# Offsets for the gate and rounding points of prepared weights, units 12 to 108

## The chip, the cores and the metric

The kernel runs on one core of one Trainium2 chip. The metric is device time in microseconds (us) for one execution. The engines that matter here are TensorE (PE, with its weight load PEld), VectorE (DVE), ScalarE (ACT), GpSimd (POOL) and SyncE (SP), which issues most of the transfers.

## The reference, cut to what matters

```python
mod = (_silu(c) @ w_mod).reshape(c.shape[0], 6, 1, -1)
sa, ca, ga, sb, cb, gb = (mod[:, i] for i in range(6))
h = _layernorm(x) * (1 + ca) + sa
q = (h @ wq).reshape(1, 2048, 32, 128)          # 32 heads, D = 576
k, v = last 512 rows of the caches, 16 heads, each used by two query heads
o = softmax(q k^T / sqrt(128)) v
x = x + ga * (o @ wo)
h = _layernorm(x) * (1 + cb) + sb
x = x + gb * (((h @ W_gate) masked where > 0) * (h @ W_up)) @ W_down      # F = 4608
```

Everything is float32 in and out.

## The kernel before

**Precision.** A float32 operand of a matmul is split into a rounded part "hi" (type fp32r) and the remainder "lo", also fp32r, and a product is three matmuls: hi·hi, lo·hi, hi·lo. So every operand costs a rounding (ACT: `scalar.copy`) and a subtraction (POOL: `tensor_sub`). The function `split` (lines 181 to 183) does this for weights; the code calls it the *cut* of a weight.

**Units.** The attention stage is a list of 128 *units*, one for each head and block of 512 queries. Eight units in a row belong to one key/value head (four blocks, two query heads); the last five key/value heads are visited twice with two blocks each, so four units in a row. TensorE works through unit u in a fixed order: the scores s of u (12 matmuls of 512 columns, L496 to L498, in the order hi·hi, lo·hi, hi·lo), the q projection of unit u+1 (14 matmuls of 512, L424), a *piece* of the output projection wo (12 matmuls of 288 columns, L660), probabilities times v for the first half of u-1 (6 of 512, L633 to L635), for the second half (6), and another wo piece (12). The other engines serve this:

- DVE: maxima of s (tile t, L501), the subtraction of the maximum (p, L591), the remainder of the next q (qlo, L480), half of the softmax sum (ks, L606), the scaling of the attention output (`o_mul`, L641, tile rb).
- ACT: the next q's rounded part (qhi, L476), the exponential (L593), the rounded p (hi, L577), the rounded output (ohi, L645).
- POOL: the rest of the softmax sum (ks, L609, two instructions), the remainder of p in two halves (lo, L600, named lo<unit>_0 and lo<unit>_1 where both halves are meant apart), the remainder of the output (olo, L649).

Each engine runs its own instructions in program order, so where a piece of side work is written decides what it stands ahead of. Within a unit POOL's fixed order is: ks of u (two instructions), lo of u (two), olo of an earlier unit (one), then ks of u+1. PE needs lo of u in the next unit's two pv halves, and olo of an odd unit, with the odd head's wo weights, in the wo piece at the end of a unit.

**Side work.** The weights of coming units are prepared meanwhile: q weights (tile wA), keys and values (kv), wo weights (raw tile roga, cut tile woga). Each has a load on SP's queue into a ring of two raw buffers, then, for wo alone, a *gate* (DVE multiplies by the row mrow, L223), then the cut (ACT copy, POOL subtraction L183). Because the raw ring has two buffers, a load is let go only when the cut two loads before it has read its buffer. Weights of the key/value heads 12 to 15 are prepared early too and parked in DRAM (`park...`), from where they are reloaded on a visit (`againq`, `againk`, `againo` in the trace). The modulation vectors are also summed beside the units, one part at a time (`m3.0` to `m5.4`, DVE, tile macc, L128 and L130).

**Their order.** Side work is not written into the unit's code. Each piece is a *step*: a name, a time and a function. Unit u is the time span 10u to 10u+9, and the unit's code calls `run(u, k)` at eleven fixed points, which executes every step whose time has come:

```python
def step(name, t, fn, *args):
    sched.append((t + PLAN.get(name, 0), len(sched), fn, args))
...
    step(name + ".l", hook(q - gap), pr[0])
    if len(pr) > 2:
        step(name + ".g", hook(q - 1), pr[1])
    step(name + ".c", t, pr[-1])
...
def run(u, k):
    t = 10 * u + k
    while sched and sched[-1][0] <= t:
        fn, args = sched.pop()[2:]
        fn(*args)
```

The suffix says which part it is: `.l` load, `.g` gate, `.c` cut (for the m steps, the summing). A name such as `q9.c` is the cut of the q weights of head 9, `k` and `v` count key/value heads, `o` the wo weights of a head. Before the change all these weights use the points 0, 4, 6 and 9 of a unit only. On POOL three gaps follow from the points: k = 6, 7, 8 falls between ks and lo of the unit (called A below), k = 9 and the next unit's 0 to 3 between lo and olo (B), and later points after olo and ahead of the next ks (C).

Of the kernel before, what the change touches and what calls it, by code (L numbers as in the profile page):

```python
# [23 lines left out]
EPS = 1e-5  # L24
SCALE = float(P) ** -0.5
H2 = D // 2
PLAN = {'a1.st0': -14, 'a1.nm0': -15, 'a1.st1': -14, 'a1.nm1': -15, 'a1.st2': -14, 'a1.nm2': -15, 'a1.st3': -14, 'a1.nm3': -15, 'a1.rs': -15, 'a1.tr0': -15, 'a1.af0': -11, 'a1.tr1': -15, 'a1.af1': -15, 'a1.tr2': -15, 'a1.af2': -15, 'mods': -3}
CFG = {'a0': (('s', 'vvp', 'vvv'), ('m', 'aap', 'avp'), ('w', 'aav')), 'a1': (('w', 'aap', 'vap'), ('m', 'vvp', 'vvv'), ('s', 'avp'))}
PE0, PE1, MLP0 = 4, 1, 8
# [5 lines left out]
def kernel(  # L35
# [106 lines left out]
    def mod_row(j, r, plus):  # L142
# [7 lines left out]
        for h in range(2):  # L150
            nc.tensor.matmul(ps[h][:, :H2], ones, m[:, h * H2:(h + 1) * H2], start=True, stop=True)
        for h in range(2):
            nc.scalar.activation(r[:, h * H2:(h + 1) * H2], ps[h][:, :H2], AF.Copy, bias=plus,
                                 scale=1.0)
# [117 lines left out]
    class LayerNorm:  # L272
# [4 lines left out]
        def stats(self, i):  # L277
# [6 lines left out]
            for h in range(2):  # L284
                nc.vector.bn_stats(bn[:, h, :], a[:, h * H2:(h + 1) * H2])
            nc.vector.bn_aggr(self.xn[-1][:, i, :], bn)
# [143 lines left out]
    def keep(key, t):  # L430
        akeep[key] = k = dr.tile(list(t.shape), F32R, name="ak%s%d" % key)
        nc.scalar.dma_start(k.bitcast(F32), t.bitcast(F32))
# [50 lines left out]
    st_, t5, pt, hi_, lo_, bc, rb, ks_, pvps, done, o, bps = ({} for _ in range(12))  # L483
# [167 lines left out]
    def down_piece(his, los, ws, i, qt, nm, pool=None, seed=None):  # L651
# [3 lines left out]
        for half in range(2):  # L655
            cs = slice(half * H2, (half + 1) * H2)
            n = 0
            for hi, lo, w in zip(his, los, ws):
                for a, b in ((hi, 0), (hi, 1), (lo, 0)):
                    nc.tensor.matmul(ps[:, half, :H2], a[:, sl], w[b][:, cs],  # L660
                                     start=(n == 0 and seed is None), stop=(n == 5),
# [4 lines left out]
        def add():  # L666
            adds[i] += 1
            if seed is not None:
                nc.scalar.copy(av, ps[:, :, :H2])
                return  # L670
# [255 lines left out]
    def w_later(s, xx, where):  # L926
        pool, tag, w = where
        st = {}
        eng = nc.gpsimd
        terms = terms_of(s, WTERMS)  # L930

        def get(dst, i, j):
            nc.sync.dma_start(dst, wlay0[i, j, :, xx, :])

        def begin():
            for x in "ab":
                st[x] = pool.tile([P, w], F32, tag=tag, name=f"w{x}_{s}_{xx}")[:, :384]
            for x, term in zip("ab", terms):
                get(st[x], *term[1:])

        def comb(i):
            x, y = st["a"], st["b"]
            eng.tensor_tensor(x, x, y, op=ALU.add if terms[i][0] == "+" else ALU.subtract)
            if i + 1 < len(terms):
                get(st["b"], *terms[i + 1][1:])

        def cut():
            a = st["a"]
            hi = st["b"].bitcast(F32R)
            nc.scalar.copy(hi, a)  # L950
            nc.gpsimd.tensor_sub(hi[0:32, 256:], a[0:32, 256:], hi[0:32, 256:].bitcast(F32))
            lo = a[:, :256].bitcast(F32R)
            nc.gpsimd.tensor_sub(lo, a[:, :256], hi[:, :256].bitcast(F32))
            stores.append((wkeep[0, s][:, xx, 0:3, :].rearrange("p t n -> p (t n)"), hi))
            stores.append((wkeep[0, s][:, xx, 3:5, :].rearrange("p t n -> p (t n)"), lo))

        return [begin] + [lambda i=i: comb(i) for i in range(1, len(terms))] + [cut]
# [326 lines left out]
    sched = []  # L1284

    def step(name, t, fn, *args):
        sched.append((t + PLAN.get(name, 0), len(sched), fn, args))

    HOOK = (0, 4, 6, 9)
    e = 10 * NU  # L1290
# [1 line left out]
    def hook(q):  # L1292
        return 10 * (q // 4) + HOOK[q % 4]

    def prep(name, t, pr, gap=2):
        q = 4 * (t // 10) + HOOK.index(t % 10)
# [4 lines that stand above are left out]
# [93 lines left out]
    step("wo1.g", 23, po[1])  # L1394
    step("wo1.c", 32, po[2])
    def sk(t, key, d, k):
        step("keep", t, lambda: keep(key, d[k][2] if key[0] == "o" else
                                     d[k] if key[0] == "q" else d[k][:, 0:8, :]))

    def weights(g, d):  # L1400

        h = 2 * g
        return [(("q", h), d["q"], prep5(d["q"], h, wq, "wA")), (("k", g), d["k"], prep_kv(d["k"], g, 0)),
                (("q", h + 1), d["q"], prep5(d["q"], h + 1, wq, "wA")),
                (("v", g), d["v"], prep_kv(d["v"], g, 1)), (("o", h), d["o"], prep_out(d["o"], h, wo, "ga")),
                (("o", h + 1), d["o"], prep_out(d["o"], h + 1, wo, "ga"))]

    live = {"q": wqs, "k": ks, "v": vs, "o": wos}
# [4 lines left out]
    for i in range(1, len(VIS)):  # L1413
        g, qbs = VIS[i]
        B = 10 * UNITS.index((g, qbs[0], 2 * g))
        if g in early or g in seen:
            for key, t in zip((("q", 2 * g), ("k", g), ("q", 2 * g + 1), ("v", g), ("o", 2 * g),
                               ("o", 2 * g + 1)), (-30, -20, -14, 0) + ((-4, -4) if i > first + 1 else (6, 34))):
                step("again", B + t, again, key, live[key[0]], key[1],
                     key[0] == "o" and key[1] % 2 and i > first and (i - first) % 2 == 0)  # L1420
        else:
            for (key, d, pr), t in zip(weights(g, live), (-31, -20, -14, 0, 9, 34)):
                prep(key[0] + str(key[1]), B + t, pr, 6 if t == 34 else 4)
                if any(v[0] == g for v in VIS[i + 1:]):
                    sk(B + t + 12, key, d, key[1])
        seen.add(g)
    for i in range(1, first):
        B = 80 * i
        for c, t, gap, a in (("q", 16, 5, 0), ("kv", 24, 5, 1), ("o", 44, 6, 2)):
            if parks[c] and i > a:  # L1430
                key, d, pr = parks[c].pop(0)
                prep("park", B + t, pr, gap)
                sk(B + t + 9, key, d, key[1])
    assert not any(parks.values())
    for i in range(15):
# [150 lines left out]
    def after(t):  # L1586
        return next(x for x in calm if x >= t)

    t = 546
    for s in ("P1", "P2", "P4", "P7", "P5", "P6", "P3"):  # L1590
        for xx in range(2):
            for fn in w_later(s, xx, (xp, "xm", 640)):
                step("w.l", t, fn)
                t = after(t + 8)
            step("w.e", t, flush_stores)
    assert t < 1040, t
# [177 lines left out]
```

## Time and profile before

| What | Value |
|---|---|
| device time, median of 3 | 2859.7 us (2857.88 to 2862.28) |
| the profiled execution: its own time | 2857.6 us |
| its span in the trace | 2855.8 us |
| granted TensorE clock, mean | 0.998 |
| PE busy | 2815.0 us, 99% |
| PEld busy | 2449.5 us, 86% |
| DVE busy | 2246.8 us, 79% |
| POOL busy | 2123.8 us, 74% |
| ACT busy | 1476.7 us, 52% |

The span covers the program's instructions; the execution's own time is 1.8 us longer. Busy shares are means over the whole program, its attention stage (units 0 to 127) and its MLP stage. A share of 99% for PE counts matmuls whose modelled ends overlap, so short waits are better seen from the starts of successive matmuls.

### The profile page before, as it was taken

The page shows a single profiled execution, that of the slowest core. Times are in us where ns is not written, and L with a number is a line of the kernel's source. Part 1 is how long each engine was busy: PE and PEld are TensorE (multiplying, and loading weights), DVE is VectorE, ACT ScalarE, POOL GpSimd, SP SyncE. Part 2 cuts the span into 40 slices and gives each one's busy share as a digit, 9 for nine tenths or more (in the row PEclk, how much of TensorE's full clock was granted, in tenths as well). Part 3 has the DMA queues.
Part 4 walks back from the last instruction along what each step waited for, and adds up shares of the span by engine and source line. Part 5 has one row for each costly group of instructions (what it writes and reads, how often), then busy time and mean ns, then how long its engine had stood idle before and what let it go on. Part 6 is the DMA issues. An engine that isn't in the chain of part 4 may idle for free.

```text
span 2855.8 us, 41174 instructions
## 1 busy us (share of the span) xinstructions
PE 2815.0 (99%) x15006; PEld 2449.5 (86%) x15006; DVE 2246.8 (79%) x3384; ACT 1476.7 (52%) x2105; POOL 2123.8 (74%) x1564
## 2 busy tenths in 40 slices
PE   6999999999999999999999999999999999999999
PEld 5788888888888888888888888888888888888888
DVE  7899999999889998888889756676677466666666
ACT  5766666666766666666656444444444122222221
POOL 5688888888899989877778766788777356656653
PEclk9999999999999999999999999999999999999999
DMA  4012132222232213312243456666667844444442
GB/s 163 24 45 79 65 106 85 83 82 100 95 104 94 92 62 131 105 70 80 68 155 139 150 213 229 231 240 231 234 234 261 338 165 154 155 155 159 159 154 106
DMA packets 164506, 399.57 MB, mean 140 GB/s; under 512 B 15056, under 2 KB 62160, under 8 KB 164304
## 3 DMA queue, kind: packets, MB, share of 16 engines
q1 hardware_dynamic: 132912, 284.69, 29.9%
q10 hardware_dynamic: 31392, 112.26, 10.0%
q8 instruction: 118, 1.93, 0.3%
q14 instruction: 84, 0.69, 0.1%
HBM read 271.16 MB, written 154.57 MB: 149 GB/s over the span
## 4 chain that ended last, share of the span: by engine, by line
PE 83%; DVE 6%; POOL 5%; issue 2%; ACT 2%; DMA 2%; SPq 0%; ACTq 0%; DVEq 0%; POOLq 0%
PE gu L1016 26%; PE wo L660 12%; PE qps L424 11%; PE md L660 8%; PE st_P L1118 6%; PE s L498 3%; PE s L497 3%; PE s L496 3%; PE pv L635 3%; PE pv L634 3%; PE pv L633 3%; POOL lo L600 2%; DVE t L501 1%; DVE p L591 1%; POOL wop L795 1%
## 5 line engine op out<-in xcount | busy, mean ns | idle before, releaser
L600 POOL TENSOR_TENSOR lo<-p,hi 128x1024 fp32r<-128x1024 f32 x256 | 610.6, 2406 | 1.1 <-ACT hi L577 1.1
L609 POOL TENSOR_TENSOR ks<-ks,p 128x512 f32<-128x512 f32 x256 | 351.7, 1374 | 238.7 <-DVE ks L606 135.5
L501 DVE TRANSPOSE_TENSOR_REDUCE t<-s 128x32 f32<-128x1024 f32 x256 | 313.8, 1239 | 85.9 <-PE s L498 76.6
L1016 PE MATMUL gu<-hop_B,wop 128*128 128x512 f32 x1512 | 375.0, 391 | 0.2 <-POOL wop L795 0.2
L1016 PEld LDWEIGHTS gu<-hop_B,wop 128*128 128x128 f32 x1512 | 274.9, 188 | 51.1 <-POOL wop L795 0.9
L1016 PE MATMUL gu<-hop_T,wop 128*128 128x512 f32 x1260 | 316.1, 391 | 0.0
L424 PE MATMUL qps<-hTa,wA 128*128 128x512 f32 x1288 | 312.9, 394 | 3.1 <-DVE hTa L372 1.6
L660 PE MATMUL wo<-woga,ohi 128*128 128x288 f32 x1472 | 298.8, 295 | 2.0 <-POOL woga L183 1.4
L591 DVE TENSOR_TENSOR p<-s,mb 128x1024 f32<-128x1024 f32 x246 | 290.3, 1219 | 4.2
L424 PEld LDWEIGHTS qps<-hTa,wA 128*128 128x128 f32 x1288 | 244.5, 190 | 56.6 <-DVE hTa L372 3.2
L476 ACT ACTIVATE qhi<-qps 128x512 fp32r<-128x512 f32 x128 | 76.4, 597 | 366.9 <-PE qps L424 358.4
L660 PEld LDWEIGHTS wo<-woga,ohi 128*128 128x128 f32 x1472 | 245.9, 188 | 18.8 <-POOL woga L183 3.4
L1016 PEld LDWEIGHTS gu<-hop_T,wop 128*128 128x128 f32 x1260 | 227.8, 188 | 39.0
L577 ACT CAST hi<-p 128x1024 fp32r<-128x1024 f32 x256 | 259.5, 1042 | 1.5
L660 PE MATMUL md<-wogb,hhi 128*128 128x288 f32 x1272 | 256.9, 295 | 0.4 <-DVE acc L671 0.4
L593 ACT ACTIVATE p<-p 128x1024 f32<-128x1024 f32 x246 | 249.5, 1051 | 13.7 <-DVE p L591 13.4
L671 DVE TENSOR_TENSOR acc<-md,acc 128x576 f32<-128x576 f32 x159 | 119.9, 755 | 160.4 <-PE md L660 159.8
L660 PEld LDWEIGHTS md<-wogb,hhi 128*128 128x128 f32 x1272 | 210.9, 188 | 12.6 <-DVE acc L671 1.4
L1127 DVE TENSOR_TENSOR acc<-st_P,acc 128x576 f32<-128x576 f32 x160 | 121.1, 757 | 127.9 <-PE st_P L1118 127.9
L660 PE MATMUL wo<-woga,olo 128*128 128x288 f32 x736 | 217.8, 296 | 1.3 <-POOL olo L649 1.2
L660 PE MATMUL md<-wogb,hlo 128*128 128x288 f32 x636 | 187.5, 295 | 0.0
L649 POOL TENSOR_TENSOR olo<-rb,ohi 128x512 fp32r<-128x512 f32 x128 | 167.4, 1308 | 15.2 <-ACT ohi L645 15.0
(283 smaller groups left out, 7095.3 us busy)
## 6 DMA issues: line engine op xcount, KB each, us to landing
wop<-wk_P SPq DMA_DIRECT2D x133, 640.0 KB
wk_P<-wop ACTq DMA_DIRECT2D x119, 640.0 KB
wr<-wlay SPq DMA_DIRECT2D x68, 384.0 KB
rogb<-wd SPq DMA_DIRECT2D x68, 288.0 KB
againq<-akq SPq DMA_DIRECT2D x18, 640.0 KB
rwA<-wq SPq DMA_DIRECT2D x32, 320.0 KB
wlay<-wg SPq DMA_DIRECT2D x36, 256.0 KB
roga<-wo SPq DMA_DIRECT2D x32, 288.0 KB
```

The costliest lines, as they stand in the source:

```text
L424: return [lambda i=i, a=a, b=b: nc.tensor.matmul(ps, a, b, start=(i == 0), stop=(i == n - 1)) for i, (a, b) in enumerate(ops)]
L501: nc.vector.tensor_reduce(t5[u][:, 2 * h:2 * h + 2, :].rearrange("p k b -> p (k b)"), t.rearrange("p k (b j) -> p (k b) j", j=32), axis=AX ...
L577: nc.scalar.copy(hi_[u, h], pt[u, h])
L591: nc.vector.tensor_tensor(p, t, bc[u][:, None, :].to_broadcast([P, 2, 512]), op=ALU.subtract)
L593: nc.scalar.activation(p, p, AF.Exp, bias=0.0, scale=1.0)
L600: nc.gpsimd.tensor_sub(lo_[u, h], pt[u, h], hi_[u, h].bitcast(F32))
L609: nc.gpsimd.tensor_tensor(ks_[u], ks_[u], p[:, j, :], op=ALU.add)
L649: nc.gpsimd.tensor_sub(olo[u], o.pop(u), ohi[u].bitcast(F32))
L660: nc.tensor.matmul(ps[:, half, :H2], a[:, sl], w[b][:, cs], start=(n == 0 and seed is None), stop=(n == 5), skip_group_check=seed is not None)
L1016: nc.tensor.matmul(ps, a, c, start=s not in heir(m) and i == 0 and s not in seeds_of(m), stop=i == len(ops) - 1, skip_group_check=True)
L1118: nc.tensor.matmul(ps[:, j, :H2], x[:, sl], w[:, y, :], start=n == 0 and not second, stop=n == 2, skip_group_check=True)
L1127: nc.vector.tensor_tensor(t, ps[:, :, :H2], t, op=ALU.add)
```

## The change

One table and one term are added. The table OFF has 103 entries, one for each of the gates and cuts of the weights prepared in units 12 to 108 and of the m3 to m5 sums; each entry moves one step by -3 to +10 tenths of a unit. Other edits of the diff give distinct names to steps (reloads, stores to DRAM, the later combinations of MLP weights) that have no entry in the table, so loads, stores, reloads and copies keep their times. No instruction is added or removed.

```diff
+OFF = {'parkq25.c': -2, 'm4.2.c': 1, 'parkq27.c': -1, 'm4.1.c': 10, 'parkq26.c': 7, 'k3.c': 2, ...
 PLAN = {'a1.st0': -14, ...
...
     def step(name, t, fn, *args):
-        sched.append((t + PLAN.get(name, 0), len(sched), fn, args))
+        sched.append((t + PLAN.get(name, 0) + OFF.get(name, 0), len(sched), fn, args))
...
-        step("keep", t, lambda: keep(key, d[k][2] if key[0] == "o" else
+        step(f"keep{key[0]}{key[1]}_{int(t >= 1000)}", t, lambda: keep(key, d[k][2] if key[0] == "o" else
...
-                step("again", B + t, again, key, live[key[0]], key[1],
+                step(f"again{i}{key[0]}{key[1]}", B + t, again, key, live[key[0]], key[1],
...
-                prep("park", B + t, pr, gap)
+                prep(f"park{key[0]}{key[1]}", B + t, pr, gap)
...
-                step("w.l", t, fn)
+                step(f"w{s}{xx}.{t}", t, fn)
```

What this does to an engine's order is seen from the instructions themselves. On POOL, in units 33 and 34 (the number after ks, lo and olo is the unit; wA_27 are the q weights of head 27, kv13_0 the keys of key/value head 13), before:

```order
L649 TENSOR_TENSOR olo31_4856<-rb31_4755,ohi31_4854 128x512
L609 TENSOR_TENSOR ks33_4881<-ks33_4881,p33_1_4871 128x512 x2
L183 TENSOR_TENSOR wA_27_4885<-rwA_27_4734,wA_27_4885 128x640
L600 TENSOR_TENSOR lo33_0_4915<-p33_0_4868,hi33_0_4874 128x1024
L600 TENSOR_TENSOR lo33_1_4917<-p33_1_4871,hi33_1_4910 128x1024
L649 TENSOR_TENSOR olo32_4923<-rb32_4877,ohi32_4921 128x512
L183 TENSOR_TENSOR kv13_0_4982<-rkv13_0_4796,kv13_0_4982 128x512
L609 TENSOR_TENSOR ks34_5010<-ks34_5010,p34_1_5000 128x512 x2
```

The same engine and place after the change (lines of the changed kernel are one higher):

```order
L650 TENSOR_TENSOR olo31_4856<-rb31_4755,ohi31_4854 128x512
L184 TENSOR_TENSOR wA_27_4871<-rwA_27_4734,wA_27_4871 128x640
L610 TENSOR_TENSOR ks33_4884<-ks33_4884,p33_1_4874 128x512 x2
L601 TENSOR_TENSOR lo33_0_4915<-p33_0_4868,hi33_0_4877 128x1024
L601 TENSOR_TENSOR lo33_1_4917<-p33_1_4874,hi33_1_4910 128x1024
L650 TENSOR_TENSOR olo32_4923<-rb32_4880,ohi32_4921 128x512
L184 TENSOR_TENSOR kv13_0_4967<-rkv13_0_4796,kv13_0_4967 128x512
L610 TENSOR_TENSOR ks34_5010<-ks34_5010,p34_1_5000 128x512 x2
```

The cut wA_27 has moved from gap A (between ks33 and lo33) to gap C (ahead of ks33).

On DVE, in unit 34 (macc4 is a part of the m4 sum, roga_9 the gate of the wo weights of head 9, rb33 the scaling `o_mul` of unit 33), before:

```order
L606 TENSOR_TENSOR ks34_5010<-p34_0_4995 128x512
L641 TENSOR_TENSOR rb33_5006<-pv33_4985,rb33_5006 128x512
L130 SCALAR_TENSOR_TENSOR macc4_3917<-wm4_3_4888,sT_133,macc4_3917 128x576
L223 TENSOR_TENSOR roga_9_4919<-roga_9_4919,mrow2_892 128x576
L501 TENSOR_REDUCE t5_35_5054<-s35_0_5047 128x32
```

And after:

```order
L607 TENSOR_TENSOR ks34_5010<-p34_0_4995 128x512
L131 SCALAR_TENSOR_TENSOR macc4_3884<-wm4_3_4888,sT_133,macc4_3884 128x576
L642 TENSOR_TENSOR rb33_5006<-pv33_4985,rb33_5006 128x512
L224 TENSOR_TENSOR roga_9_4919<-roga_9_4919,mrow2_892 128x576
L502 TENSOR_REDUCE t5_35_5054<-s35_0_5047 128x32
```

The two side instructions stood in a row; now `o_mul` stands between them.

On POOL, in units 42 and 43 (kv13_1 are the values of key/value head 13, woga_11 the wo weights of head 11), before:

```order
L183 TENSOR_TENSOR kv13_1_5984<-rkv13_1_5800,kv13_1_5984 128x512
L609 TENSOR_TENSOR ks42_6012<-ks42_6012,p42_1_6002 128x512 x2
L600 TENSOR_TENSOR lo42_0_6043<-p42_0_5997,hi42_0_6005 128x1024
L600 TENSOR_TENSOR lo42_1_6045<-p42_1_6002,hi42_1_6038 128x1024
L649 TENSOR_TENSOR olo41_6110<-rb41_6008,ohi41_6108 128x512
L183 TENSOR_TENSOR woga_11_6112<-roga_11_5921,woga_11_6112 128x576
L609 TENSOR_TENSOR ks43_6139<-ks43_6139,p43_1_6129 128x512 x2
```

And after:

```order
L610 TENSOR_TENSOR ks42_6009<-ks42_6009,p42_1_5999 128x512 x2
L184 TENSOR_TENSOR kv13_1_6033<-rkv13_1_5800,kv13_1_6033 128x512
L601 TENSOR_TENSOR lo42_0_6043<-p42_0_5994,hi42_0_6002 128x1024
L601 TENSOR_TENSOR lo42_1_6045<-p42_1_5999,hi42_1_6038 128x1024
L184 TENSOR_TENSOR woga_11_6077<-roga_11_5921,woga_11_6077 128x576
L650 TENSOR_TENSOR olo41_6113<-rb41_6005,ohi41_6111 128x512
L610 TENSOR_TENSOR ks43_6139<-ks43_6139,p43_1_6129 128x512 x2
```

Here kv13_1 has moved from ahead of ks42 (C) into gap A of unit 42, and woga_11 from behind olo41 to ahead of it (from C to B).

## Rows read from the trace of the kernel before

**Rows 1.** Timeline of PE, unit 99: start us, busy us, engine, instruction.

```profile
1248.43 0.39 PE L496 MATMUL s<-qhi,againk 128*128 128x512 f32 x1
...
1260.25 0.39 PE L496 MATMUL s<-qhi,againk 128*128 128x512 f32 x1
```

**Rows 2.** Timeline of PE, first matmuls of units 12 and 108.

```profile
193.91 0.39 PE L496 MATMUL s<-qhi,kv 128*128 128x512 f32 x1
...
1344.13 0.39 PE L496 MATMUL s<-qhi,againk 128*128 128x512 f32 x1
```

**Rows 3.** Waits of PE, units 12 to 106: us in total, times, longest.

```profile
PE wo L660 <- POOL woga L183: 1.4, 3, 0.7
PE wo L660 <- POOL olo L649: 1.2, 5, 0.5
PE pv L635 <- POOL lo L600: 1.1, 2, 0.6
PE s L498 <- DVE qlo L480: 0.7, 1, 0.7
```

**Rows 4.** Groups of PE by line, units 12 to 107: busy us, mean ns, idle before.

```profile
L171 PE MATMUL mps<-ones,macc 128*128 128x1 f32 x20 | 2.3, 242 | 0.0
L151 PE MATMUL mps<-macc5b,ones 128*128 128x288 f32 x4 | 1.3, 431 | 0.0
```

**Rows 5.** Timeline of POOL, unit 99 to 100: in brackets idle before, and its releaser.

```profile
1260.24 2.67 POOL L609 TENSOR_TENSOR ks<-ks,p 128x512 f32<-128x512 f32 x2 [3.17 <-DVE ks L606]
...
1268.12 1.29 POOL L649 TENSOR_TENSOR olo<-rb,ohi 128x512 fp32r<-128x512 f32 x1 [0.50 <-ACT ohi L645]
```

**Rows 6.** Timeline of DVE, end of unit 99.

```profile
1258.85 0.65 DVE L480 SCALAR_TENSOR_TENSOR qlo<-qps,qhi 128x512 fp32r<-128x512 f32 x1
1259.43 0.67 DVE L606 TENSOR_TENSOR ks<-p 128x512 f32<-128x512 f32 x1
...
1261.84 1.25 DVE L501 TRANSPOSE_TENSOR_REDUCE t<-s 128x32 f32<-128x1024 f32 x1 [1.14 <-PE s L498]
```

**Rows 7.** Timeline of POOL, units 34 and 35.

```profile
466.68 1.32 POOL L183 TENSOR_TENSOR kv<-rkv,kv 128x512 fp32r<-128x512 f32 x1
468.68 3.06 POOL L609 TENSOR_TENSOR ks<-ks,p 128x512 f32<-128x512 f32 x2 [0.69 <-DVE ks L606]
...
478.20 1.42 POOL L183 TENSOR_TENSOR woga<-roga,woga 128x576 fp32r<-128x576 f32 x1
```

**Rows 8.** Timeline of PE, unit 35, to the first matmul of unit 36.

```profile
468.38 0.39 PE L496 MATMUL s<-qhi,kv 128*128 128x512 f32 x1
...
479.67 0.40 PE L660 MATMUL wo<-woga,ohi 128*128 128x288 f32 x1 [0.36 <-POOL woga L183]
...
480.85 0.39 PE L496 MATMUL s<-qhi,kv 128*128 128x512 f32 x1
```

**Rows 9.** Timeline of DVE, units 34 and 35.

```profile
467.56 0.98 DVE L606 TENSOR_TENSOR ks<-p 128x512 f32<-128x512 f32 x1
...
469.06 1.53 DVE L130 SCALAR_TENSOR_TENSOR macc<-wm,sT,macc 128x576 f32<-128x576 f32 x1
470.52 1.84 DVE L223 TENSOR_TENSOR roga<-roga,mrow 128x576 f32<-128x576 f32 x1
```

**Rows 10.** Timeline of DVE, unit 32: a gate while POOL stands idle.

```profile
444.50 0.75 DVE L223 TENSOR_TENSOR roga<-roga,mrow 128x576 f32<-128x576 f32 x1
```

**Rows 11.** Timeline of POOL, unit 33: the subtraction of wA_27.

```profile
459.18 1.57 POOL L183 TENSOR_TENSOR wA<-rwA,wA 128x640 fp32r<-128x640 f32 x1
```

**Rows 12.** Timelines of SP and DVE: load and gate of one wo weight.

```profile
373.23 2.52 SPq L219 DMA_DIRECT2D roga<-wo  x1
...
386.11 1.54 DVE L223 TENSOR_TENSOR roga<-roga,mrow 128x576 f32<-128x576 f32 x1
```

**Rows 13.** Timelines of SP and PE, unit 95: a reload and the matmul behind it.

```profile
1196.01 0.80 SPq L445 DMA_DIRECT2D againo<-ako  x2
...
1199.81 0.53 PE L660 MATMUL wo<-againo,ohi 128*128 128x288 f32 x2 [0.29 <-DMA againo<-ako]
```

More of the change, by code (lines that the diff above doesn't have):

```diff
@@ L26 @@
 H2 = D // 2
+OFF = {'parkq25.c': -2, 'm4.2.c': 1, 'parkq27.c': -1, 'm4.1.c': 10, 'parkq26.c': 7, 'k3.c': 2, 'k5.c': 10, 'q9.c': -3, 'parko25.g': -3, 'q8.c': 5, 'o4.c': 6, 'o5.g': 3, 'q11.c': 9, 'q7.c': 4, 'q5.c': -3, 'parkk13.c': -2, 'm3.3.c': -3, 'v2.c': -3, 'o7.g': -1, 'q10.c': 4, 'o3.c': -2, 'parko25.c': -3, 'parko24.g': -1, 'm4.3.c': -2, 'q4.c': 4, 'm3.2.c': 1, 'm4.0.c': -3, 'v4.c': 4, 'k2.c': 1, 'o9.g': -1, 'm3.1.c': 1, 'o8.c': 1, 'parko24.c': -1, 'o6.g': 1, 'parkk12.c': -3, 'm3.4.c': -1, 'v3.c': 2, 'k4.c': 4, 'o6.c': 2, 'm4.4.c': -2, 'q6.c': 4, 'q12.c': 1, 'parkv13.c': 3, 'k7.c': 2, 'o15.c': -3, 'parkv14.c': 3, 'v5.c': 3, 'k6.c': 4, 'o13.g': -3, 'q13.c': -3, 'o12.g': 1, 'v7.c': 2, 'q14.c': 6, 'parko28.c': -2, 'v6.c': 1, 'o11.c': -3, 'o14.c': 4, 'parkq30.c': 1, 'o10.g': 1, 'parko26.g': -1, 'm5.3.c': 1, 'm5.1.c': -3, 'o15.g': -1, 'q15.c': 5, 'parko27.c': -2, 'parko28.g': -3, 'parko26.c': -3, 'o13.c': -3, 'm5.4.c': -3, 'parko27.g': -1, 'parkq28.c': -1, 'parkq29.c': 2, 'v10.c': 7, 'q21.c': 8, 'o20.c': 6, 'o17.g': -3, 'o19.c': -2, 'parko30.g': -3, 'q20.c': 10, 'parko31.g': -2, 'q17.c': -3, 'o16.c': -1, 'v9.c': 2, 'k10.c': 10, 'parkv15.c': -1, 'parko30.c': -2, 'k8.c': 8, 'o20.g': 2, 'q19.c': 7, 'q18.c': 2, 'parko29.c': 1, 'parkq31.c': -2, 'o16.g': 2, 'parkk15.c': -1, 'v8.c': 2, 'o18.c': 1, 'o18.g': 3, 'k11.c': -1, 'o22.g': -1, 'o22.c': 5, 'q23.c': -1, 'q22.c': 5, 'o23.c': -1}
 PLAN = {'a1.st0': -14, 'a1.nm0': -15, 'a1.st1': -14, 'a1.nm1': -15, 'a1.st2': -14, 'a1.nm2': -15, 'a1.st3': -14, 'a1.nm3': -15, 'a1.rs': -15, 'a1.tr0': -15, 'a1.af0': -11, 'a1.tr1': -15, 'a1.af1': -15, 'a1.tr2': -15, 'a1.af2': -15, 'mods': -3}
```

## The prediction, made before the changed kernel had run

> **What bounds the kernel now.** The page's busy shares come first: PE 99% at a granted clock of 0.998, so the clock takes nothing and only PE's waits can give time back. An order of side work can change nothing else, as no instruction is added or removed. The timeline of PE gives the scale. In an undisturbed unit PE runs without a pause, 1260.25 - 1248.43 = 11.82 us [rows 1]. Units 12 to 107, which hold every moved step, take 1344.13 - 193.91 = 1150.22 us [rows 2]; 96 times 11.82 is 1134.7. So 15.5 us are above the floor. Of these 2.3 + 1.3 = 3.6 us are small matmuls that belong to the modulation and stay [rows 4], and about 0.5 is a wait for a reload, which the change doesn't touch [rows 13]. **At most 11.4 us can be won.**
>
> The view of PE's waits says what ends them: the wo weights' cut, olo, lo and qlo, in the ratio 1.4 : 1.2 : 1.1 : 0.7 [rows 3]. Its sum of 4.4 is less than 11.4 because it counts only what remains after the modelled end of the matmul before, and drops waits too short to show. Unit 35 shows this: the row's idle time is 0.36, the unit's length 480.85 - 468.38 = 12.47, 0.65 over the floor [rows 8]. Split in that ratio, 11.4 us are 3.6 for the wo cut, 3.1 for olo, 2.9 for lo and 1.8 for qlo. Read start to start, as in unit 35, they lie in some 22 units, with 0.05 to 1.4 us in each. All are late side effects: nothing is late in a unit without side work, where lo ends at 1267.62 (the releaser's 0.50 us of idle before olo), 7.37 us after the unit's start at 1260.25, and olo at 9.16 [rows 1, 5], while in unit 35 PE missed the wo cut only at 479.67 - 0.36 - 468.38 = 10.9 us [rows 8].
>
> **The prices.** A POOL cut takes 1.32 (kv), 1.42 (woga) or 1.57 us (wA) [rows 7, 11]. POOL has a gap of 3.17 us before ks of the next unit [rows 5], but its end is fixed: DVE's half of ks comes first. A DVE gate takes 0.75 us where POOL is idle [rows 10] and 1.84 where it is not, a macc 1.53 [rows 9]; DVE's own room is the 1.14 us before t [rows 6]. So there are two ways to be late: a cut that pushes lo or olo on POOL, or a pair of side instructions on DVE.
>
> The last also works backwards. DVE's ks takes 0.67 us undisturbed [rows 6], but in unit 34 a kv cut ran on POOL from 466.68 to 468.00 and ks took 0.98 us; POOL's ks then waited 0.69 us for it and started at 468.68, 0.3 after the unit's start at 468.38 instead of at it [rows 7, 8, 9]. So a cut in gap C, behind olo and ahead of ks, is free only if it ends before DVE wants ks, 0.82 us ahead of the unit's start [rows 1, 6].
>
> The Trainium skill (SBUF — State Buffer, Who interferes with whom) says that the two engines share a port pair, locked for a whole instruction, and that a DVE instruction with two SBUF inputs contends with a GpSimd instruction that reads SBUF. The trace agrees in the 0.98 for 0.67 just named. By that rule alone ks could be held by a whole wA cut, and moves into C would return most of what they free.
>
> **The change part by part.**
>
> *Units 33 to 36, the place shown.* Before, wA_27 (1.57) runs between ks33 and lo33, so lo33 and olo32 are 1.57 late, kv13_0 runs into DVE's ks34, and POOL's ks34 is 0.3 late. On DVE macc (1.53) and gate (1.84) stand in a row where POOL is busy; together 3.4 us against a room of 1.14. The wo cut ends at 479.62 and PE waits [rows 7, 8]. After, wA_27 stands ahead of ks33, in C. It starts behind olo31 and holds DVE's ks33 by up to its length less the room, which I put at 0.7 to 1.0 us late for ks33 instead of 1.57 for lo33. Then kv13_0 ends before DVE's ks34, macc goes ahead of o_mul where POOL is idle (0.75), and the gate alone stays behind it. The wo cut comes some 0.35 earlier, and DVE is no longer late for qlo36. Gain: 0.35 in unit 35, 0.45 in 36, and by the same pair of DVE instructions parted, 0.45 in 37.
>
> *Units 42 to 45.* In 44 to 45 the same pair (macc and a gate) goes apart: the 1.4 us of unit 45, qlo and olo together, go. But in 42 kv13_1 now stands between ks42 and lo42, and woga_11 ahead of olo41. Counted from the unit's start: ks to 2.67, kv to 3.97, two lo to 8.7 (2.37 each as in [rows 5]), with some contention 9.1, woga to 10.5, olo to 11.8. PE wants it by about 10.9. So 0.9 us are lost where 0.2 stood before. Net gain 0.7.
>
> *The other places*, walked through with the same prices: wA or woga no longer ahead of the late instruction in units 59 (0.7), 66 (0.65), 81 and 85 (0.4 each) and 75 (0.2); seven small ones (17, 18, 23, 47, 51, 61, 69) give 0.07 to 0.16 each, 0.8 together. Losses: units 27 (0.1), 67 (0.2), where the cut now ends later; 82 and 89 (0.3 each), where a gate now stands between DVE's subtractions p of one unit and qlo is late. Unchanged: 12, 19, 50 and 58, 1.8 us in all, since what stands ahead there isn't moved far enough.
>
> *Sum.* Gains 0.35 + 0.45 + 0.45 + 0.7 + 0.7 + 0.65 + 0.4 + 0.4 + 0.2 + 0.8 = 5.1, losses 0.9, so **-4.2 us**. That is 37% of the 11.4. The profiled execution's own 2857.6 becomes 2853.4; the median of three runs, 2859.7, lies 2.1 higher and would become 2855.5. Between the two I say **2854.5**. ACT's casts move with the cuts and are hidden: ACT is busy 52%. Stores, loads and reloads keep their issue points on every queue.
>
> **What I don't know.** How long ks is held by a cut in C: between nothing (the cut ends in time) and 1.57 plus the rest of DVE's ks. Twelve cuts are moved there (units 14, 17, 26, 33, 41, 46, 53, 65, 68, 79, 81, 86). I take half, since the row nearest shows 0.3 us for a cut that overlapped by 0.44 (467.56 to 468.00) [rows 7, 9]. At nothing the sum is about -8, at the full length about 0.
>
> **The rivals.**
>
> *B: nearly all the waits go.* If cuts in C are mostly in time, and units 42, 82 and 89 have room that I don't see, 9 to 11 of the 11.4 us go: 2848 to 2850. For it: POOL's gap of 3.17 us holds a wA cut twice [rows 5]. Against: four places hold the same instructions as before, 1.8 us, and three new ones look late.
>
> *C: the stall moves to ks.* The cut that leaves A for C holds DVE's ks for its full length, POOL's ks and lo start as late as before, and only the parted DVE pairs (units 36, 37, 45) gain, while 27, 43, 67, 82 and 89 lose about as much. Sum 0 to -1.5: 2857 to 2860. For it: 0.98 instead of 0.67 in unit 34 [rows 9].
>
> *D, the other side: a load waits for a later cut.* The raw ring has two buffers, so a load is let go by the cut two loads before. Where that cut is moved later (parkq26.c by 7 points ahead of the load of o7; also q20 ahead of q21, and five more), the load goes later, while o7's gate is moved 1 earlier. My walk through the timelines of POOL and DVE in units 26 and 27 leaves 2.4 to 3.2 us between the freed load of o7 and the point at which DVE comes to its gate, an estimate. What a load takes the trace bounds from two sides: a reload with PE waiting for it took 1199.81 - 1196.01 = 3.8 us [rows 13], and a wo weight issued at 373.23 was there when its gate ran at 386.11, so at most 12.9 [rows 12]. At 3.8 DVE is 1 us late, inside its room of 1.14 before t and of the 0.75 by which qlo is ready ahead of the next unit (1260.25 less 1259.50) [rows 1, 6], 1.9 together: nothing. At 12.9 it is 10 us late, and PE loses some 8.2: 2857.6 - 4.2 + 8.2 = 2861.6, with a second such place in part 2865. It decides from a landing of about 2.8 + 1.9 + 4.2 = 8.9 us. Against: the nearest row is the 3.8.
>
> **How the numbers follow.** A change of 0.2%, 5.7 us, is about what a measurement of this kernel can tell from none. Chances: my forecast (-2 to -8) 0.5, B 0.16, C 0.22, D 0.12. The forecast's own range is 2849.5 to 2857.5, from both bounds of the unknown and both bases. For the whole, leaving out half of B below and most of D above: 2848.5 to 2861. Faster by over 0.2%: all of B and half of the forecast's -2 to -8, 0.42. Slower: the upper part of D and a little of C, 0.11. The same: 0.47.
>
> **What would show it.** In the changed kernel's timeline of PE, units 36, 37, 45, 59, 81 and 85 should last 11.8 to 11.9; unit 35 some 12.1; unit 43 should be 12.6 or more with a wait for olo; 58 should still be 0.8 over. The waits of PE should sum to some 2.8 instead of 4.4. For C, DVE's ks in the units with a cut in C would average far over 0.67 and lo would start late; for D, a gate would wait for a load on DVE in unit 27. The forecast is wrong if time is gained outside units 12 to 107, or if units 36, 45 and 59 keep their length.

## The result and the profile after

The changed kernel takes 2864.51 us (median of 15; 2859.7 to 2872.62) against 2859.46 (2855.21 to 2865.22): a ratio of 1.0019, 95% interval 1.0012 to 1.0027, so 3.4 to 7.7 us **slower**. Forecast was 2854.5 with a range up to 2861, and a chance of 0.47 that nothing measurable changes, 0.42 for faster and 0.11 for slower. The profiled execution took 2864.51 us, its span 2862.7, 6.9 more than before.

Where did it go? First matmul of unit 12 to first of unit 108, the stretch that holds every moved step:

| Stretch | before, us | after, us |
|---|---|---|
| units 12 to 107 | 1150.22 | 1150.59 |
| of these, 27 to 29 | 35.74 | 38.61 |
| of these, 35 to 37 | 37.02 | 35.75 |
| of these, 43 to 45 | 37.11 | 36.46 |
| of these, 59 | 12.75 | 14.31 |
| unit 127's first matmul to the end | 1275.95 | 1281.55 |

Two things stand out. The gains in the units are there, but units 27 to 29 and 59 ate them. And 5.6 us were added from unit 127 to the end, where no step was moved.

PE's waits in units 12 to 106 (us in total, times, longest) answer to [rows 3]:

```profile
PE s L499 <- DVE qlo L481: 2.4, 2, 1.9
PE wo L661 <- POOL olo L650: 1.7, 4, 0.8
PE pv L636 <- POOL lo L601: 1.4, 3, 0.7
PE s L497 <- DVE p L592: 0.4, 1, 0.4
```

The wait for the wo cut (1.4 before) is gone from the list, the one for qlo has grown from 0.7 to 2.4. Its longest, 1.89, is in unit 28, and the chain behind it is short. Timelines of SP, DVE and PE in the changed kernel:

```profile
372.51 0.33 SPq L220 DMA_DIRECT2D roga<-wo  x1
```

```profile
377.30 2.74 DVE L224 TENSOR_TENSOR roga<-roga,mrow 128x576 f32<-128x576 f32 x1 [2.42 <-POOL ks L610]
```

```profile
389.28 0.50 PE L499 MATMUL s<-qlo,kv 128*128 128x512 f32 x1 [1.89 <-DVE qlo L481]
```

The load of o7 now goes at 372.51 us, right behind the cut that frees its buffer; before the change it went at 365.99. Its gate waits 2.42 us on DVE and then takes 2.74 instead of 0.75, because POOL's lo has begun meanwhile:

```profile
377.03 5.27 POOL L601 TENSOR_TENSOR lo<-p,hi 128x1024 fp32r<-128x1024 f32 x2
```

DVE never catches up within the unit. The profile names POOL's ks as releaser; the experiments below show that it is the load.

The 5.6 us behind the units lie mostly at one place. The view of PE's waits over the whole span of the changed kernel has a new entry near its top:

```profile
PE md L661 <- DVE acc L672: 2.4, 1, 2.4
```

DVE and POOL there, in the changed kernel (L824 sums two blocks of MLP weights, L795 and L796 cut others):

```profile
1978.80 0.69 DVE L1214 SCALAR_TENSOR_TENSOR c<-c 128x512 f32<-128x512 f32 x1
1979.41 6.07 DVE L824 TENSOR_TENSOR wr<-wr,wr 128x768 f32<-128x768 f32 x1
1985.40 0.75 DVE L672 TENSOR_TENSOR acc<-md,acc 128x576 f32<-128x576 f32 x1
```

```profile
1979.34 0.74 POOL L795 TENSOR_TENSOR wop<-wr,wop 32x256 fp32r<-32x256 f32 x1 [1.83 <-ACT wop L794]
1980.05 1.29 POOL L796 TENSOR_TENSOR wop<-wr,wop 128x512 fp32r<-128x512 f32 x1
1981.31 1.42 POOL L184 TENSOR_TENSOR wogb<-rogb,wogb 128x576 fp32r<-128x576 f32 x1
1982.70 1.28 POOL L1157 TENSOR_TENSOR hlo<-c,hhi 128x512 fp32r<-128x512 f32 x1
1983.94 0.71 POOL L795 TENSOR_TENSOR wop<-wr,wop 32x256 fp32r<-32x256 f32 x1
1984.62 1.97 POOL L796 TENSOR_TENSOR wop<-wr,wop 128x512 fp32r<-128x512 f32 x1
```

The same place in the kernel before, DVE and then POOL:

```profile
1977.77 0.95 DVE L823 TENSOR_TENSOR wr<-wr,wr 128x768 f32<-128x768 f32 x1
```

```profile
1977.97 1.34 POOL L794 TENSOR_TENSOR wop<-wr,wop 32x256 fp32r<-32x256 f32 x1 [1.83 <-ACT wop L793]
```

Before, DVE's sum starts 0.20 us ahead of POOL's cut and takes 0.95 us. After, POOL is 0.07 us ahead (1979.34 against 1979.41), works without a pause through five instructions, and DVE's sum takes 6.07 us. PE, which wants the next accumulation, waits 2.4 us, and then its clock is lower for a while. Busy times by stretch (PE, PEld, DVE, ACT, POOL, then granted clock, DMA share, GB/s):

```profile
1982.00:1986.00 4.00, 1.79 (x8) 1.14 (x7) 4.00 (x2) 1.10 (x2) 4.00 (x4) 1.00 0.99 356
1986.00:1989.20 3.20, 3.00 (x12) 3.00 (x13) 1.61 (x3) 1.45 (x2) 2.33 (x3) 0.50 0.69 280
```

A granted clock of 0.50 is the lower of its two levels, 1.2 GHz; it followed a stretch in which PE was busy 1.79 of 4 us. With it PE is 4.2 us behind the quickest profile at the same matmul, and 3.5 us of that are left a few us later. A second wait, 1.4 us near 2239 us for a reload of MLP weights, adds most of the rest; of the other profiles only that of after_pad6 has it at that size (2.5 us). The last 0.56 us lie behind PE's last matmul, in the closing semaphore instructions: from its start to the end of the span it is 4.74 us in both profiles of the changed kernel, against 4.18 before (4.16 in off_empty, below).

### The profile page after: what moved, and what is told of

Its sections match the earlier page's. It is cut to its first block, busy times and chain, and to the rows that moved or that the text cites. A ratio compares the mean times of both kernels' runs of the same rounds, so it can differ in the third digit from the quotient of the medians.

```text
span 2862.7 us, 41157 instructions
## 1 busy us (share of the span) xinstructions
PE 2815.8 (98%) x15006; PEld 2450.5 (86%) x15006; DVE 2250.1 (79%) x3384; ACT 1473.9 (51%) x2105; POOL 2123.2 (74%) x1564
## 4 chain that ended last, share of the span: by engine, by line
PE 84%; DVE 5%; POOL 4%; ACT 2%; DMA 2%; issue 2%; SPq 0%; ACTq 0%; POOLq 0%; DVEq 0%
PE gu L1017 25%; PE wo L661 12%; PE qps L425 12%; PE md L661 7%; PE st_P L1119 6%; PE s L499 4%; PE s L498 4%; PE s L497 4%; PE pv L636 3%; PE pv L635 3%; PE pv L634 3%; POOL lo L601 1%; POOL wop L796 1%; DVE ws L824 1%; DVE p L592 1%
```

## What could shift POOL by a quarter of a microsecond

In the MLP stage the two programs have the same instructions. POOL's lead over DVE can be followed back to one cast on ACT, some 12 us earlier. Timeline of ACT, before:

```profile
1964.96 0.35 ACTq L752 DMA_DIRECT2D wk_P<-wop  x1
1965.63 0.83 ACT L793 CAST wop<-wr 128x768 fp32r<-128x768 f32 x1 [1.57 <-DVE acc L671]
...
1968.56 0.35 ACTq L752 DMA_DIRECT2D wk_P<-wop  x1
1968.95 0.84 ACT L793 CAST wop<-wr 128x768 fp32r<-128x768 f32 x1
```

And after:

```profile
1966.61 0.35 ACTq L753 DMA_DIRECT2D wk_P<-wop  x1
1967.01 0.83 ACT L794 CAST wop<-wr 128x768 fp32r<-128x768 f32 x1 [1.12 <-POOL wop L796]
...
1969.93 0.35 ACTq L753 DMA_DIRECT2D wk_P<-wop  x1
1970.60 0.84 ACT L794 CAST wop<-wr 128x768 fp32r<-128x768 f32 x1 [0.31 <-ACT hhi L1156]
```

From the start of the DMA issue to the cast behind it, 0.67 us pass in one case and 0.40 in the other, and this changes places: before, the first pair is slow and the second quick (0.39), after, the other way round. The profile names DVE's acc as the releaser of the slow cast before, but that came 0.20 us ahead of the cast's start, where the quick cast starts 0.03 us behind its own. So ACT makes a pause of about 0.3 us that no semaphore explains, and the change moved it to the next cast. Counting all of ACT's records from the program's start, issues and semaphore instructions included, such pauses stand at numbers 2111, 2495 and 3135 in the profile of before, and at 2367, 2495 and 2751 in that of after. They differ by multiples of 64; not every such record shows one. ACT has 3223 records before and 3217 after: moved steps need their waits in another order, and so the program needs 6 semaphore instructions fewer on ACT. (The page's head counts them on all engines:)

```profile
span 2855.8 us, 41174 instructions
```

```profile
span 2862.7 us, 41157 instructions
```

The cast near 1965 us is record 2495 before, where the pause falls, and 2489 after, where none does. Record 2495 starts 0.32 us after the end of record 2494 in all fourteen profiles of this document, whether it is a cast or a DMA issue. And the cast sets POOL's start: POOL's cut near 1979 us starts 12.29 to 12.34 us after it in all fourteen, while DVE's sum starts 12.12 to 12.14 after it where the pause falls on the cast, and 12.40 to 12.42 where it doesn't.

Theories, as the expectations below name them. **A**: units 27 to 29 and 59 are the real loss, the rest is chance of single profiles. **B**: the MLP stage really is longer after the change; **B'**, formed after the first four runs: by ACT's pause, as just told. **C**: any shift of the start or of addresses would do. (These letters are not those of the prediction's rivals.)

## The experiments

Each ran in five rounds beside the kernel before. Kernels with a table of their own are the changed kernel with other entries.

**1. off_empty.** Edit: `OFF = {}`.

> The table is empty, so this is the kernel before under the changed text. Both theories: ratio 1.000 within 0.1%; units 12 to 107 take 1150 us. Its second use: how much the MLP stage differs from one profile of the same order to the next. Theory A (the 5 us outside the units are chance of one profile): the MLP stage here differs by up to some us from the first profile of before. Theory B (the MLP stage really is longer after the change): it repeats within 1 us.

Measured: ratio 1.000 (0.9990 to 1.0009); units 12 to 107 take 1149.65 us. From unit 127 on it took 1279.48, 3.5 more than the first profile: the sum of the same line one round earlier, near 1909 us, took 6.07 us here and held PE for 2.4. That place goes either way by chance: PE lost over 2.5 us there in 5 of all 14 profiles, with both orders. So a single profile's MLP stage can be 3.5 us off, as theory A has it.

**2. after_again.** No edit.

> The changed kernel once more. Theory A: units 12 to 107 again 0.4 us longer than before (o7's wait 2.9, units 58 and 59 1.6, against gains of some 6 elsewhere), the MLP stage within 2 us of before's, and the time over before by less than 2 us. Theory B: the MLP stage again 4 to 5 us longer with a wait of PE for acc, and the time 5 us over before.

Measured: ratio 1.0017 (1.0008 to 1.0027), so the loss repeats. Units 12 to 107 took 1147.22 us: unit 59 is 12.03 here, as forecast, so its 14.31 was chance (in every version it swings, 12.2 to 12.8 with the order of before; DVE's ks waits there for a buffer that a transfer still reads). But the wait near 1983 us is there again, with DVE's sum at 6.07. From unit 127 on it took 1280.50, of which 2.6 us are the chance wait near 1909 us. A falls by the time, B stands.

**3. mend_o7_59.** Five entries less:

```diff
-'parkq26.c': 7, 'o7.g': -1, 'parkv14.c': 3, 'o15.c': -3, 'o15.g': -1
```

> The changed table without the five entries of the two places that went wrong (parkq26.c, o7.g; parkv14.c, o15.c, o15.g). Theory A: units 12 to 107 4 us shorter than before, near the forecast, and the time 4 us under before. Theory B: the units are 4 us shorter too, but the MLP stage stays 4 to 5 us longer, and the time is that of before or 1 us over.

Measured: ratio 1.0004 (0.9992 to 1.0015). Units 12 to 107 take 1145.47 us, 4.75 less than in the first profile of before, and the time is still that of before: as B said.

**4. only_o7.** Two entries alone: `OFF = {'parkq26.c': 7, 'o7.g': -1}`.

> The kernel before with two entries alone: the cut of parkq26 7 tenths later and the gate of o7 1 earlier. If the load that waits for the later cut is the cause, units 27 and 28 are 2.9 us longer, with DVE waiting about 2.4 us ahead of the gate, and the time is 3 us over before (theory A) or more if a shift of the MLP stage adds to it (theory B). If the wait before the gate is not the load's, nothing changes.

Measured: ratio 1.0006 (0.9996 to 1.0016), 1.7 us, inside its own error. The units show it without one: 27 to 29 take 38.74 us instead of 35.74. Timelines of DVE (two stretches) and of SP in this kernel:

```profile
376.16 0.81 DVE L224 TENSOR_TENSOR roga<-roga,mrow 128x576 f32<-128x576 f32 x1 [2.00 <-DMA roga<-wo]
```

```profile
388.97 1.23 DVE L224 TENSOR_TENSOR roga<-roga,mrow 128x576 f32<-128x576 f32 x1 [1.60 <-DMA roga<-wo]
```

```profile
371.78 0.33 SPq L220 DMA_DIRECT2D roga<-wo  x1
372.16 0.58 SPq L1460 DMA_DIRECT2D wlay<-wg  x1
372.79 3.37 SPq L1460 DMA_DIRECT2D wlay<-wu  x1
376.27 5.83 SPq L220 DMA_DIRECT2D roga<-wo  x1
```

Here the releaser is the transfer, by name. There are two waits, not one: o7's load lands 4.4 us after its issue, and the next wo weight, issued behind the wlay copies at 376.27, lands 12.7 us after its issue began (388.97), 1.6 late; the issue alone held SP for 5.83 of them. Most of the loss in only_o7, 2.5 us in unit 29, comes from the second. The same holds in after_again and after_pad12; in the first profile after the change and in after_pad6 the first load does it, with 2.25 and 3.9 us in unit 28.

**5 to 7. Six copies on ACT.** Tiny copies bring ACT's count back to that of before (after_pad6, mend_pad6), or move it off (before_pad6):

```diff
     nc.scalar.activation(sT, cT, AF.Exp, bias=0.0, scale=-1.0)
+    for _ in range(6):
+        nc.scalar.copy(cp.tile([P, 1], F32, tag="pad", name="pad"), mhalf[:, 0:1])
```

> The changed kernel with six tiny copies (128x1) on ACT while ACT is idle at the start. The order of the change leaves ACT with 6 instructions fewer ahead of the MLP stage; the pause of 0.2 to 0.3 us that the traces show on ACT at every 64th place or so then falls on another instruction. Theory B' (that shift lets POOL start 0.1 us ahead of DVE near 1979 us, DVE's sum is held 6 us, and PE waits): with 3225 instructions on ACT as before, the wait near 1983 us is gone, DVE's sum there takes 0.95 us instead of 6.07, the MLP stage is 2.7 to 4 us shorter, and the time is 2 over before instead of 5. Theory A (chance of single profiles): the wait comes or not as it likes, and the time stays 5 us over before.

Measured: ratio 1.0003 (0.9995 to 1.0012), and the wait near 1983 us is gone. The profiled MLP stage is not shorter, though: from unit 127 on it took 1281.14 us, with a wait of 2.5 us for a reload near 2234. So the gain rests on the times of all executions, not on this profile. DVE's sum in this kernel:

```profile
1976.70 0.95 DVE L826 TENSOR_TENSOR wr<-wr,wr 128x768 f32<-128x768 f32 x1
```

> The mended table with the same six copies. Theory B': units 12 to 107 at 1145.5, MLP stage as before, time 4 us under before. Theory A: as the mended table without the copies, the time of before.

Measured: ratio 0.9988 (0.9979 to 0.9997), 3.4 us under before; units 1145.66; DVE's sum 0.95. Its profile, the slowest of the kernel's eleven executions, has the chance wait near 1909 us and takes 1281.40 from unit 127 on, not the time of before.

> The kernel before with the same six copies, so that the pause on ACT moves off the cast near 1965 us. Theory B': POOL is 0.27 us earlier there, DVE's sum near 1979 us takes 6 us, PE waits 2.5 us, and the time is 3 to 4 us over before, though no step of the attention stage is moved. Theory A: no difference.

Measured: DVE's sum takes 6.07 us and PE loses 2.7 there at its worst and 2.05 in the end, though no step is moved; but the ratio is 0.9999 (0.9990 to 1.0008). The place behaved as B' said, the time didn't.

**8. best_pad.** Eight entries less than the changed kernel, and five copies:

```diff
-'parkq26.c': 7, 'o7.g': -1, 'parkv14.c': 3, 'o15.c': -3, 'o15.g': -1, 'parkv13.c': 3, 'o11.c': -3, 'o22.g': -1
```

> The mended table without three more entries (parkv13.c and o11.c of units 42 and 43, o22.g of unit 88), with five copies on ACT so that ACT again has 3225 instructions. Theory B': units 12 to 107 at 1144.4 and the time 5 to 6 us under before. Theory A: units the same, time within 2 us of before.

Measured: 2853.52 us, ratio 0.9985 (0.9976 to 0.9993), **4.3 us under before**: faster than both kernels. Units 12 to 107 take 1144.09. PE's waits in them:

```profile
PE pv L638 <- POOL lo L603: 0.6, 1, 0.6
PE wo L663 <- POOL woga L186: 0.4, 1, 0.4
...
PE wo L663 <- POOL olo L652: 0.2, 1, 0.2
```

**9 to 12. The counter-test.** Twelve copies instead of six put the pause six records ahead of the cast; no copies leave best_pad's table at 3218 records (the expectations count two more than the traces show: 3225 and 3220).

> The changed kernel with twelve tiny copies on ACT instead of six. If the six helped because they put ACT's pause back on the cast near 1965 us (theory B'), twelve don't: the pause falls six instructions ahead of it, DVE's sum near 1980 us takes 6 us again, and the time is 5 us over before, as without copies. If any shift of the start or of addresses helped (theory C), twelve do as well as six: 1 us over before.

Measured: ratio 1.0021 (1.0012 to 1.0030). Twelve copies don't help. DVE's sum here:

```profile
1977.11 6.07 DVE L826 TENSOR_TENSOR wr<-wr,wr 128x768 f32<-128x768 f32 x1
```

> The mended table with twelve copies. Theory B': DVE's sum near 1977 us takes 6 us, time that of before (six copies gave 3.4 us under). Theory C: 3 us under before.

Measured: ratio 1.0005 (0.9996 to 1.0014), DVE's sum 6.07. C falls twice.

> The table without eight entries, with no copies: 3220 instructions on ACT. Units 12 to 107 at 1144. Theory B': DVE's sum near 1976 us takes 6 us and the time is 0 to 1 us under before, where the same table with the copies gave 4.3 us under. Theory C, or chance: about 4 us under, as with the copies.

Measured: ratio 0.9995 (0.9986 to 1.0004), DVE's sum 6.05, units 1144.39.

> The kernel before with six copies, once more, since its wait near 1981 us came as theory B' says but its time did not rise. Theory B': the wait comes again, and the time is 2.5 us or more over before. If the time is that of before again, other waits of the MLP stage get shorter with the same shift, and the 4 to 5 us that the copies are worth in the changed kernel are not that one wait alone.

Measured: DVE's sum 6.07 again, ratio 1.0005 (0.9996 to 1.0014). Both runs of this kernel together: 0.6 us over before, with an error of about 1.8.

All fourteen profiles at the two places:

| Kernel | cast's record on ACT | DVE's sum, us | units 27 to 29, us | units 12 to 107, us | unit 127 to the end, us | ratio |
|---|---|---|---|---|---|---|
| before | 2495 | 0.95 | 35.74 | 1150.22 | 1275.95 | 1 |
| off_empty | 2495 | 0.95 | 35.72 | 1149.65 | 1279.48 | 1.0000 |
| before_pad6 | 2501 | 6.07 | 35.78 | 1149.60 | 1277.88 | 0.9999 |
| before_pad6b | 2501 | 6.07 | 35.73 | 1149.26 | 1278.54 | 1.0005 |
| only_o7 | 2495 | 0.95 | 38.74 | 1152.43 | 1275.95 | 1.0006 |
| after | 2489 | 6.07 | 38.61 | 1150.59 | 1281.55 | 1.0019 |
| after_again | 2489 | 6.07 | 37.66 | 1147.22 | 1280.50 | 1.0017 |
| after_pad6 | 2495 | 0.95 | 40.21 | 1150.89 | 1281.14 | 1.0003 |
| after_pad12 | 2501 | 6.07 | 37.63 | 1147.31 | 1284.48 | 1.0021 |
| mend_o7_59 | 2489 | 6.07 | 35.70 | 1145.47 | 1278.67 | 1.0004 |
| mend_pad6 | 2495 | 0.95 | 35.75 | 1145.66 | 1281.40 | 0.9988 |
| mend_pad12 | 2501 | 6.07 | 35.75 | 1146.08 | 1284.00 | 1.0005 |
| best_pad | 2495 | 0.95 | 35.73 | 1144.09 | 1276.51 | 0.9985 |
| best_pad0 | 2490 | 6.05 | 35.75 | 1144.39 | 1279.24 | 0.9995 |

The pause falls on record 2495. Where that is the cast, POOL comes late and DVE's sum is free, six times of six; where not, it is held, eight times of eight. The stretch from unit 127 on does not sort that way, since the waits near 1909 and 2234 us come into it by chance; what the pause is worth must be read from the times.

## Why the prediction was wrong

**The step that failed** is the second sentence on what bounds the kernel: "An order of side work can change nothing else, as no instruction is added or removed." No compute instruction is, but 17 others go, 6 of them on ACT. They moved a pause of 0.3 us in the MLP stage onto another cast, which lost DVE a race with POOL and PE 2.0 to 3.7 us, counted where PE has its clock back. By times it is worth 4.0 to 5.1 us with the changed table (1.0019, 1.0017 and 1.0021 against 1.0003), 4.6 to 4.9 with the mended one (1.0004 and 1.0005 against 0.9988) and 2.9 with the last (0.9995 against 0.9985), each with an error of 3 to 4 us, so that the last alone is not clear of noise. The working looked for the end of each moved step inside units 12 to 107 and gave the rest no term at all, and no rival named it. The trace of before had such a held sum to show, near 1819 us, where it is in all fourteen profiles: DVE came 0.66 us behind POOL, and the sum ended only after POOL had run out of work at 1822.02. Timelines of DVE and POOL, before:

```profile
1819.46 3.38 DVE L823 TENSOR_TENSOR wr<-wr,ws 128x768 f32<-128x768 f32 x1
```

```profile
1818.80 0.72 POOL L794 TENSOR_TENSOR wop<-wr,wop 32x256 fp32r<-32x256 f32 x1 [1.31 <-ACT wop L793]
1819.49 1.28 POOL L795 TENSOR_TENSOR wop<-wr,wop 128x512 fp32r<-128x512 f32 x1
1820.74 1.28 POOL L867 TENSOR_TENSOR hx_B<-hx_B,hy_B 128x512 fp32r<-128x512 f32 x1
```

**The second step** is rival D's size. Its mechanism, a load let go by a later cut, was right, and so was the place, o7. The sum had given 3.8 us of landing the price "nothing"; 4.4 us cost 3.0 in only_o7. The walk stopped at o7's own gate. The next wo load stands behind it on SP's queue, among the wlay copies, and its gate was late too. It is the load of [rows 12], whose 12.9 us the prediction had only as an upper bound for o7's; once it had to be waited for, it took 12.7. With both entries units 27 to 29 took 1.9 to 4.5 us longer in all five profiles, without them no more than 0.04.

**The sum over the units was right.** The mended table lacks o7's two entries and the three of unit 59, so its forecast is -4.2 without the loss of 0.1 in unit 27 and the gain of 0.7 in 59: -3.6. The three mended profiles average 1145.7 us, the four with before's order 1149.7: -3.9. By place: unit 35 gained 0.37 (0.35 forecast), 36 0.45 (0.45), 37 0.46 (0.45), 43 to 45 0.65 (0.7), 66 0.74 (0.65), 81 and 85 0.4 each (0.4 each), 75 0.11 (0.2); 82 and 89 lost 0.36 and 0.32 (0.3 each), 67 nothing (0.2). Unit 58 kept its length (12.68), as forecast. Unit 43 waits for olo as worked out: olo ended 11.7 us after the unit's start at 567.71 (11.8 forecast). Timelines of POOL and of PE in the changed kernel:

```profile
576.73 1.44 POOL L184 TENSOR_TENSOR woga<-roga,woga 128x576 fp32r<-128x576 f32 x1
578.12 1.30 POOL L650 TENSOR_TENSOR olo<-rb,ohi 128x512 fp32r<-128x512 f32 x1
```

```profile
579.47 0.40 PE L661 MATMUL wo<-woga,olo 128*128 128x288 f32 x1 [0.59 <-POOL olo L650]
```

Unit 59's gain of 0.7 can't be judged: its chance swing is as large.

**Rival C fell, and the half that was taken for it was enough.** The sign that the prediction named for it did come: in the twelve units with a cut moved to gap C, DVE's ks takes 1.58 us on average (0.96 to 2.09) against 0.73 before. That is a hold of 0.85, near the half of 1.57 that was taken, and the sum over the units came out as worked out with it. Over units 12 to 106 the mean is 856 ns against 755. The group of ks in the changed kernel (busy us, mean ns, idle before):

```profile
L607 DVE TENSOR_TENSOR ks<-p 128x512 f32<-128x512 f32 x95 | 81.3, 856 | 2.7 <-ACT hi L578 2.4
```

By the rule of the Trainium skill (SBUF — State Buffer, Who interferes with whom) whoever issues first has the shared port pair for one whole instruction. The ks of the units agree: the longest, 2.09 us, is 1.42 over its undisturbed 0.67, no more than one cut (1.28 to 1.57 in the rows). The sum in the MLP stage, held through five instructions of POOL, does not fit it.

What adds up: units -0.7 with o7's losses (the four profiles of the changed table average 1149.0), and for the pause +4.0 to 5.1 by the times, together some 4 us, within the 3.4 to 7.7 measured. Counted from the traces alone it is less: -0.7, 2.0 to 3.7 at the held sum and 0.56 at the program's end make 1.9 to 3.6. The rest of the 5.05 us between the medians, 1.5 to 3.2, is accounted for by no place that repeats.

**What stays open.** Where the rest of the loss lies, if it is not noise. Why the kernel of before_pad6 shows the wait in both its profiles (at 1983.71 and 1985.65 us) and yet no loss in time: so the pause is shown to cost time with the changed and the mended table, and not with before's order. A wait that comes by chance elsewhere may have become rarer with that shift: the one near 1909 us was in neither of its profiles, but two profiles don't show it. The copies also act elsewhere: units 108 to 126 take 0.3 us less in all seven profiles with copies (235.4 to 235.5 against 235.7 to 235.8). Also open is what the pause on ACT is. The Trainium skill (Runtime: NRT & Kernel Launch, Instruction fetch mechanics) has instructions streamed in blocks of 256, at a cost that is mostly hidden. The trace's step of 64 differs from that, and no run here shows that a fetch causes it.

## What to carry to other kernels

A reordering that adds no work can still change the number of semaphore instructions, and with them everything that is timed to a tenth of a microsecond later in the program: compare the stages that were not touched as carefully as the one that was, and take more than one profile before putting a loss down to chance. When a cut is moved, ask which load its buffer releases, and which loads stand behind that one on the same queue. The parts of such a table are worth separating: one pair of entries, o7's, cost 1.9 to 4.5 us where the mended table gained 3.9.

## What the runs showed of the hardware

- ACT paused about 0.3 us without a semaphore that explains it, at records whose numbers differ by multiples of 64; record 2495 came 0.32 us after the one before it in all fourteen profiles.
- DVE's sum of two SBUF tiles (128x768) takes 0.95 us if it starts ahead of POOL's cut, and 6.05 to 6.07 if POOL is 0.07 to 0.12 us ahead and stays busy: it got in only at POOL's sixth instruction. Near 1819 us, where POOL works through three instructions and stops, it takes 3.38. In the attention stage DVE's ks was held for no more than about one instruction of POOL (0.96 to 2.09 us for 0.67).
- In only_o7 a wo load took 4.4 us from issue to the gate that waited for it. The next one took 12.7, of which its own issue held SP for 5.83, behind a copy on the same queue that had held SP for 3.37.
